# State @ W in two wide visits per batch, one x load on another queue, token sums on VectorE: a cross-attention plus GLU kernel on one core

## The chip, the cores and the metric

One core of a Trainium2 chip. The metric is the device time of one execution in microseconds (us), as the median of several executions. The profile's span is some 1.8 us shorter than the device time of the same execution (before: 232.0 for 233.72). TensorE is called PE in the profile, VectorE DVE, ScalarE ACT, GpSimd POOL, SyncE SP; PEld is the load of weights into TensorE.

## The reference, cut to what matters

```
# x: (8 batches, 8 heads, 512 tokens, 64), state: (8, 8, 32, 64), all float32
a     = softmax(x @ state.T / 8)          # each token over the 32 states
xread = a @ state
a2    = softmax(state @ x.T / 8)          # each state over the 512 tokens
sread = a2 @ x
y     = concat(xread, sread)  ->  (8 * 544, 512)
out   = (sigmoid(y @ w_gate) * (y @ w_val)) @ w_out     # 512 -> 1536 -> 512
```

The kernel uses two identities. First, xread @ W = a @ (state @ W): so it makes SW = state @ W of a batch (a small matmul, 64x32 tiles of the array, eight at a time) and multiplies it by aT. Second, both softmaxes share E = exp(x @ state.T / 8); the second one needs sums of E over the 512 tokens ("token sums").

## The kernel before: what the change touches

In the loop over batches, `b - 1` is at its output matmuls (`out_mm`), `b` at gate and value (`gv_mm`), and `nb = b + 1` is prepared: S and E, aT, token sums and sread (`sr_mm`), and SW (`sw_visit` on TensorE, `sw_cp` out of PSUM). PSUM has eight banks: gv 2, out 1 (`OU`), swp 4, attention 1 (`AT`). Names in code and traces: `xb` is x of a batch in bf16 and `xT` its transpose, which S needs; `ab` is the softmax a and `aT` its transpose, which gate and value multiply by SW; `res` is a block of out copied out of PSUM for its store. S is the product x @ state.T, E its exponential, sr the product for sread.

```python
    def sr_mm(b, place):                       # token sums, then sread, in one bank
        ...
        for e in range(2):
            for c in range(4):                 # 8 matmuls: 4 token groups x 2 head halves
                nc.tensor.matmul(sm, ones[:, e], Eb[:, c, e], start=(e == 0 and c == 0), stop=(e == 1 and c == 3))
        ... # 16 matmuls of sread

    def gv_mm(b, f, place):                    # 2 banks of gv: gate, value
        ... # 2 x 2 matmuls 128x512; then th = tanh(gate / 2) on ACT, glu = (th + 1) * value on DVE

    ... # start-up: batches 0 and 1, all weights and x of 0 to 3
    load_x(2, nc.gpsimd)
    load_wo(0); load_wo(1); load_wo(2)         # (three lines)
    ...
    pad(2, 6)
    load_x(3, nc.sync, 1, nc.gpsimd)           # SP, held until GpSimd gets here
    cast_x(2, pool, 0, 4)
    cast_x(2, pool, 4, 4)
    cast_x(3, pool, 0, 4)
    cast_x(3, pool, 4, 4)
    at_xT_dma(2)                               # 4 DMA transposes each, on SP
    at_xT_dma(3)

    for b in range(1, B + 1):
        nb = b + 1 if b + 1 < B else None
        if b == 1:
            for i in range(2):
                S_mm(nb, i, (AT, GV)[i])       # waits for the transposes of batch 2
                S_exp(nb, i)
                n_sum(nb, i)
                n_mul(nb, i, nc.vector)
            aT_dma(nb)
        for f in range(NF):                    # NF = 12
            if b < B or f < 9:
                out_mm(b - 1, f)
            if b > 1:
                gv_mm(b, f, SWP if b == B and f % 2 else GV)
                gv_th(b, f)
                gv_glu(b, f)
            if nb is not None:
                lo, q = f // 4 * 512, f % 4
                if q == 0:
                    sw_visit(nb, lo, 512, 0, 1)            # f = 0, 4, 8: four swp banks
                sw_cp(nb, lo, q // 2, q % 2, act)          # all twelve copies on ACT
                if f < 2 and b > 1:
                    S_mm(nb, f, AT)
                    S_exp(nb, f)
                elif f == 5:
                    sr_mm(nb, AT)
                    sr_fin(nb)
                ...
```

The softmax here doesn't subtract the row's maximum and nothing guards it: scores larger than these inputs give would overflow.

## Time and profile before

| | before |
|---|---|
| time, median (lowest to highest) of the first 4 executions | 233.35 us (232.95 to 233.52) |
| TensorE busy | 95% of the span |
| DVE, ACT, POOL busy | 52%, 60%, 18% |
| loop period (first visit of one batch to that of the next) | 24.11, 24.18, 24.26, 24.18 us |
| lost before the loop, waiting for transposes of batch 2 | 2.3 us |

The period is read from the starts of the first state @ W matmul of each batch in the timeline: 62.84, 86.95, 111.13, 135.39, 159.57. A timeline line reads: start, duration, engine, line of the kernel, operation, tile written <- tiles read, shape, how many; in brackets the idle time in front of it and what ended it.

### The profile page before, as it was taken

To read this page: it belongs to the slowest core of one execution; us is meant where nothing else is said; L and a number is where in the kernel's file an instruction comes from. 1 tells how busy PE (TensorE), PEld (TensorE's weight loads), DVE (VectorE), ACT (ScalarE), POOL (GpSimd) and SP (SyncE) were. 2 spreads that over 40 slices of the span, in tenths; PEclk is the share of its full clock that TensorE was granted. 3 is DMA by queue.
4 is the path that set the end of the run, shared out by engine and by line. 5 is a ranking of instruction groups with operands and counts; after the bars stand their busy time and mean duration, and the time that the engine had idled before them with its cause. 6 is when DMAs were issued, how large, how long until landed. Compare 5 with 4: busy or idle time off the path is not lost.

```text
span 232.0 us, 4595 instructions
## 1 busy us (share of the span) xinstructions
PE 220.8 (95%) x1784; PEld 110.9 (48%) x1784; DVE 120.3 (52%) x198; ACT 138.5 (60%) x258; POOL 42.6 (18%) x76
## 2 busy tenths in 40 slices
PE   7668999889999999999999999999999999999994
PEld 7553445344444444444445444544454444466754
DVE  2599889852157435753486339533763343332311
ACT  3677786555775677666765676567756644422411
POOL 1499720330041003300150006000200000000000
PEclk9799999999999999999999999999999999999999
DMA  6999999952956460644172721153113111112114
GB/s 210 351 185 186 251 246 243 137 105 45 269 157 188 105 148 29 212 102 118 45 226 54 129 94 45 37 124 113 48 34 103 48 45 45 45 61 77 45 33 107
DMA packets 38790, 28.09 MB, mean 121 GB/s; under 512 B 20976, under 2 KB 34160, under 8 KB 38768
## 3 DMA queue, kind: packets, MB, share of 16 engines
q1 hardware_dynamic: 33600, 22.49, 36.5%
q0 software_dynamic: 5024, 5.24, 13.3%
q8 instruction: 14, 0.23, 0.4%
q14 instruction: 8, 0.07, 0.1%
q10 hardware_dynamic: 144, 0.07, 0.1%
HBM read 18.35 MB, written 8.91 MB: 118 GB/s over the span
## 4 chain that ended last, share of the span: by engine, by line
PE 84%; DMA 6%; DVE 4%; SPq 3%; POOL 1%; issue 0%; DVEq 0%
PE outp L274 37%; PE gvp L246 31%; PE swp L212 5%; PE gvp L249 5%; DMA xf<-in_x_dram 4%; SPq L124 3%; DMA xT<-xb 3%; DVE ab L156 2%; PE Sp L130 1%; PE srp L193 1%; PE srp L190 1%; PE outp L293 1%; DVE rs L148 1%; POOL xb L99 1%; DVE ri L150 0%; SPq L78 0%
## 5 line engine op out<-in xcount | busy, mean ns | idle before, releaser
L261 DVE SCALAR_TENSOR_TENSOR glu<-th,gvp 128x512 bf16<-128x512 f32 (+1 forms) x108 | 70.2, 656 | 87.6 <-ACT th L256 68.5
L274 PE MATMUL outp<-wo,glu 128*128 128x512 bf16 x396 | 99.6, 379 | 0.0
L246 PE MATMUL gvp<-aT,SW 128*128 128x512 bf16 x384 | 96.5, 379 | 0.1
L256 ACT ACTIVATE th<-gvp 128x512 f32<-128x512 f32 (+1 forms) x108 | 61.4, 573 | 54.7 <-PE gvp L246 45.4
L246 PEld LDWEIGHTS <-SW 128*128 128x128 bf16 x384 | 37.0, 98 | 45.7 <-issue 2.8
L274 PEld LDWEIGHTS <-glu 128*128 128x128 bf16 x396 | 36.5, 98 | 43.2 <-issue 5.6
L232 ACT CAST SW<-swp 128x512 bf16<-128x512 f32 (+1 forms) x90 | 50.3, 580 | 6.0 <-PE swp L212 5.3
L278 ACT ACTIVATE res<-outp 128x512 f32<-128x512 f32 x33 | 19.7, 597 | 19.5 <-PE outp L274 19.5
L141 POOL CAST Eb<-E 128x256 bf16<-128x256 f32 x32 | 12.4, 429 | 101.8 <-ACT E L135 101.8
L99 POOL CAST xb<-xf 128x1024 bf16<-128x1024 f32 (+1 forms) x13 | 14.6, 1148 | 18.5 <-DMA xf<-in_x_dram 13.3
L156 DVE TENSOR_TENSOR ab<-E,ri 128x512 bf16<-128x512 f32 x14 | 14.7, 1051 | 0.1
L148 DVE TENSOR_REDUCE rs<-E 128x16 f32<-128x512 f32 x16 | 10.8, 676 | 2.3 <-ACT E L135 2.3
L135 ACT ACTIVATE E<-Sp 128x512 f32<-128x512 f32 x16 | 9.6, 609 | 2.7 <-PE Sp L130 2.6
L212 PE MATMUL swp<-wg,sTc 64*32 64x512 bf16 (+1 forms) x208 | 10.4, 369 | 0.0
L212 PE MATMUL swp<-wv,sTc 64*32 64x512 bf16 (+1 forms) x208 | 10.0, 361 | 0.2 <-POOL wv L90 0.2
L199 DVE RECIPROCAL r<-srp 128x128 f32<-128x128 f32 x8 | 7.6, 956 | 3.5 <-PE srp L193 3.5
L130 PE MATMUL Sp<-sTz,xT 128*128 128x64 bf16 x128 | 7.1, 198 | 2.5 <-DMA xT<-xb 1.6
L212 PEld LDWEIGHTS <-sTc 64*32 64x32 bf16 x416 | 4.1, 89 | 10.6 <-issue 10.1
L130 PEld LDWEIGHTS <-xT 128*128 128x128 bf16 x128 | 5.7, 101 | 6.9 <-issue 2.4
L249 PE MATMUL gvp<-XS,wg 128*128 128x256 bf16 x48 | 7.2, 273 | 0.0
L249 PE MATMUL gvp<-XS,wv 128*128 128x256 bf16 x48 | 7.2, 273 | 0.0
L307 PE MATMUL warm<-ident 128*128 128x128 bf16 x56 | 5.8, 290 | 1.4 <-POOL ident masks.py:199 1.4
(50 smaller groups left out, 92.3 us busy)
## 6 DMA issues: line engine op xcount, KB each, us to landing
out_dram<-res SPq DMA_DIRECT2D x31, 256.0 KB, 2.5
xf<-in_x_dram SPq DMA_DIRECT2D x6, 1024.0 KB, 6.7
wo<-in_moe_w_out_dram POOLq DMA_DIRECT2D x3, 512.0 KB, 17.7
xf<-in_x_dram SPq DMA_DIRECT2D x2, 512.0 KB, 5.4
wg<-in_moe_w_gate_dram POOLq DMA_DIRECT2D x2, 512.0 KB, 7.1
wv<-in_moe_w_val_dram POOLq DMA_DIRECT2D x2, 512.0 KB, 7.9
xf<-in_x_dram POOLq DMA_DIRECT2D x1, 1024.0 KB, 10.1
out_dram<-res SPq DMA_DIRECT2D x9, 64.0 KB, 1.7
```

Of the source, the lines that this page charges most:

```text
L99: cp(xbs[b].rearrange("p c h d -> p h c d")[:, lo:lo + n], xfs[b][:, lo:lo + n])
L130: nc.tensor.matmul(ps[:, c, :, jj], xTs[b][:, 2 * i + jj, c], sTz[:, b, 2 * i + jj], start=True, stop=True)
L148: nc.vector.tensor_reduce(rs, halfE(b, i), AX.X, ALU.add)
L156: eng.tensor_tensor(abs_[b].rearrange("p c e (j n) -> p (c e) j n", n=Ns)[:, :, 2 * i:2 * i + 2], halfE(b, i), ri.unsqueeze(3).to_broadcas ...
L212: nc.tensor.matmul(pss[e][j * Ns:(j + 1) * Ns, o:o + n], sTc[rows, b, j], (wg, wv)[w][rows, j, lo:lo + n], start=True, stop=True)
L232: cp(*sw_left.pop((b, lo, w, e)))
L246: nc.tensor.matmul(ps, SWs[b][:, g, w, fs], aTs[b][:, :, g], start=(g == 0), stop=(g == 1))
L249: nc.tensor.matmul(ps, (wg, wv)[w][:, j, fs], XS[:, j], start=(j == 0), stop=(j == 3))
L256: nc.scalar.activation(th, held["gv", b, f][0], AF.Tanh, scale=0.5)
L261: nc.vector.scalar_tensor_tensor(glus[b][:, f], held["th", b, f], 1.0, held["gv", b, f][1], ALU.add, ALU.mult)
L274: nc.tensor.matmul(ops[b, c], glus[b][:, f, c * 128:(c + 1) * 128], wo[:, f], start=(f == 0), stop=(f == NF - 1))
L278: nc.scalar.activation(res, ops[b, c], AF.Copy, scale=0.5)
```

## The change

Intent: TensorE is the bound, so give it less. Two visits of six banks in place of three of four save one change into and out of the tiled mode a batch; sums over the four token groups are added on DVE in fp32 and go to TensorE as two bf16 terms (value and remainder), so 4 matmuls in place of 8; x of batch 3 goes by ACT's DMA queue, so that SP's queue is free for the transposes.

```diff
+    def n_tok(b, e):
+        if e == 0:
+            held["E4", b] = ap_.tile((128, 2, 4, Ns), FP, name="E4")
+        nc.vector.tensor_reduce(held["E4", b][:, e].rearrange("p j n -> p (j n)"),
+                                E1s[b][:, :, e].rearrange("p c j n -> p (j n) c"), AX.X, ALU.add)
+    def n_split(b, k):
+        if k == 0:
+            Es[b] = ap_.tile((128, 2, 2, 4, Ns), BF, name="Es")
+            nc.vector.tensor_copy(Es[b][:, 0], held["E4", b])
+        else:
+            nc.vector.tensor_tensor(Es[b][:, 1], held["E4", b], Es[b][:, 0], ALU.subtract)
 ...  sr_mm: 4 terms from Es where there is one (batches 2 to 7)
+    def sw_wide(b, v):
+        ...
+        lo = 768 * v
+        for k, places in enumerate(((OU, AT), (SWP, SWP), (SWP, SWP))):
+            ...  k = 0: gate, 512 columns; k = 1: value, 512; k = 2: 256 of each
 ...
     gv_mm(1, 1, GV)
+    load_x(3, nc.scalar)
     gv_th(1, 1)
 ...
-    load_x(3, nc.sync, 1, nc.gpsimd)
 ...  in the loop:
+            v, q = f // 6, f % 6
+            if nb is not None and q == 0:
+                sw_wide(nb, v)                 # f = 0 and 6, ahead of gv_mm, and gv_mm ahead of out_mm
+                sw_cp(nb, v, 0, 0, act)
+                sw_cp(nb, v, 0, 1, act)
 ...  copies: two of the twelve on DVE; S at f = 1, 2; n_tok at 6, 7; n_split at 7, 8; sr_mm at 9; sr_fin at 10
 ...  out of batch 0 in the two gv banks, as OU is taken
```

More of the change, by code (lines that the diff above doesn't have):

```diff
@@ L65 @@
     xfs, xbs, xTs = {}, {}, {}
-    E1s, Ebs, abs_, aTs, SWs, glus = {}, {}, {}, {}, {}, {}
+    Es, E1s, Ebs, abs_, aTs, SWs, glus = {}, {}, {}, {}, {}, {}, {}
     vec, act, pool = nc.vector.tensor_copy, nc.scalar.copy, nc.gpsimd.tensor_copy
@@ L187, in sr_mm @@
         sr, sm = sr_parts(b)
-        for e in range(2):
-            for c in range(4):
-                nc.tensor.matmul(sm, ones[:, e], Eb[:, c, e], start=(e == 0 and c == 0), stop=(e == 1 and c == 3))
+        if b in Es:
+            terms = [(e, Es[b][:, k, e]) for e in range(2) for k in range(2)]
+        else:
+            terms = [(e, Eb[:, c, e]) for e in range(2) for c in range(4)]
+        for i, (e, rhs) in enumerate(terms):
+            nc.tensor.matmul(sm, ones[:, e], rhs, start=(i == 0), stop=(i == len(terms) - 1))
         for j in range(4):
@@ L194, in sr_mm, with sr_inv @@
                                  Eb[:, c, :, j], start=(c == 0), stop=(c == 3))
+    def sr_inv(b):
+        r2 = held["r2", b] = ap_.tile((128, 4, Ns), FP, name="r2")
+        nc.vector.reciprocal(r2, sr_parts(b)[1])
     def sr_fin(b):
-        sr, sm = sr_parts(b)
-        r2 = ap_.tile((128, 4, Ns), FP, name="r2")
-        nc.vector.reciprocal(r2, sm)
+        if ("r2", b) not in held:
+            sr_inv(b)
+        sr, r2 = sr_parts(b)[0], held["r2", b]
         for e in range(2):
@@ L229, in sw_visit @@
                 sw_left[b, lo, w, e] = (SWs[b][:, e, w, lo:lo + n], pss[e])
+    def sw_wide(b, v):
+        if b not in SWs:
+            SWs[b] = fp.tile((128, 2, 2, dff), BF, name="SW", bufs=2)
+        lo = 768 * v
+        for k, places in enumerate(((OU, AT), (SWP, SWP), (SWP, SWP))):
+            pss = [p[0].tile((128, 512), FP, name="swp", tag=p[1]) for p in places]
+            if k < 2:
+                sw_mm(pss, b, k, lo, 512, 0)
+            else:
+                for w in range(2):
+                    sw_mm(pss, b, w, lo + 512, 256, 256 * w)
+            for e in range(2):
+                if k < 2:
+                    sw_left[b, v, k, e] = (SWs[b][:, e, k, lo:lo + 512], pss[e])
+                else:
+                    sw_left[b, v, k, e] = (SWs[b][:, e, :, lo + 512:lo + 768], pss[e].rearrange("p (w n) -> p w n", w=2))
     def sw_cp(b, lo, w, e, cp):
@@ L270, in out_mm @@
         if f0 == 0:
-            place = SWP if b == B else GV if b == 0 and c % 2 else OU
+            place = SWP if b == B else GV if b == 0 else OU
             ops[b, c] = place[0].tile((128, 512), FP, name="outp", tag=place[1])
@@ L539 @@
         for f in range(NF):
-            if b < B or f < 9:
-                out_mm(b - 1, f)
-            if b > 1:
-                gv_mm(b, f, SWP if b == B and f % 2 else GV)
-                gv_th(b, f)
-                gv_glu(b, f)
+            v, q = f // 6, f % 6
[3 more added lines that the diff above has]
+                sw_cp(nb, v, 0, 1, act)
+            for first in (nb is not None and q == 0, nb is None or q > 0):
+                if first and b > 1:
+                    gv_mm(b, f, SWP if b == B and f % 2 else GV)
+                    gv_th(b, f)
+                    gv_glu(b, f)
+                elif not first and (b < B or f < 9):
+                    out_mm(b - 1, f)
             if nb is not None:
-                lo, q = f // 4 * 512, f % 4
                 if q == 0:
-                    sw_visit(nb, lo, 512, 0, 1)
-                sw_cp(nb, lo, q // 2, q % 2, act)
-                if f < 2 and b > 1:
-                    S_mm(nb, f, AT)
-                    S_exp(nb, f)
-                elif f == 5:
+                    sw_cp(nb, v, 1, 0, vec)
+                elif q in (1, 3, 4):
+                    k = {1: 3, 3: 4, 4: 5}[q]
+                    sw_cp(nb, v, k // 2, k % 2, act)
+                if f in (1, 2) and b > 1:
+                    S_mm(nb, f - 1, AT)
+                    S_exp(nb, f - 1)
+                elif f in (6, 7):
+                    n_tok(nb, f - 6)
+                    if f == 7:
+                        n_split(nb, 0)
+                elif f == 8:
+                    n_split(nb, 1)
+                elif f == 9:
                     sr_mm(nb, AT)
+                    sr_inv(nb)
+                elif f == 10:
                     sr_fin(nb)
-                    if b > 1 and nb + 1 < B:
+                if f in (2, 4) and b > 1:
+                    n_sum(nb, f // 2 - 1)
+                elif f in (3, 5) and b > 1:
+                    n_mul(nb, f // 2 - 1, nc.vector)
+                if f == 3:
+                    at_Eb(nb)
+                    if nb + 2 < B:
+                        load_x(nb + 2, nc.sync)
+                elif f == 5 and b > 1:
+                    aT_dma(nb)
+                    if nb + 1 < B:
                         cast_x(nb + 1, pool, 0, 4)
@@ L560 @@
                         at_xT_dma(nb + 1)
-                if f in (1, 3) and b > 1:
-                    n_sum(nb, f // 2)
-                elif f in (2, 4) and b > 1:
-                    n_mul(nb, f // 2 - 1, nc.vector)
-                if f == 2:
-                    at_Eb(nb)
-                    if nb + 2 < B:
-                        load_x(nb + 2, nc.sync)
-                elif f == 4 and b > 1:
-                    aT_dma(nb)
     for k in range(6):
```

## The prediction

> **What bounds the kernel now.** I began with the page: engine shares, then the chain that ended last.
>
> ```profile
> PE 220.8 (95%) x1784; PEld 110.9 (48%) x1784; DVE 120.3 (52%) x198; ACT 138.5 (60%) x258; POOL 42.6 (18%) x76
> PEclk9799999999999999999999999999999999999999
> PE 84%; DMA 6%; DVE 4%; SPq 3%; POOL 1%; issue 0%; DVEq 0%
> ```
>
> TensorE is busy 95% of the span at full clock and is 84% of the chain, so from about 50 us on the end moves by what TensorE is given or spared. Because a busy matmul row is a modelled length, I price TensorE by distances between starts, from the timeline. One batch in the middle (TensorE rows only):
>
> ```profile
> 156.89 1.03 PE L246 MATMUL gvp<-aT,SW 128*128 128x512 bf16 x4
> 157.75 1.03 PE L274 MATMUL outp<-wo,glu 128*128 128x512 bf16 x4
> 158.62 1.03 PE L246 MATMUL gvp<-aT,SW 128*128 128x512 bf16 x4
> 159.57 0.41 PE L212 MATMUL swp<-wg,sTc 64*32 64x512 bf16 x8
> 159.80 0.40 PE L212 MATMUL swp<-wv,sTc 64*32 64x512 bf16 x8
> 160.13 0.41 PE L130 MATMUL Sp<-sTz,xT 128*128 128x64 bf16 x8
> 160.38 0.81 PE L274 MATMUL outp<-wo,glu 128*128 128x512 bf16 x3
> ...
> 169.91 0.61 PE L190 MATMUL srp<-Eb,ones 128*128 128x128 bf16 x8
> 170.35 0.63 PE L193 MATMUL srp<-Eb,xb 128*128 128x64 bf16 x16
> 170.82 1.03 PE L274 MATMUL outp<-wo,glu 128*128 128x512 bf16 x4
> ```
>
> Four 128x512 matmuls take 0.865 us (157.75 to 158.62). The gv block at 158.62 would end at 158.62 + 0.865 = 159.485, but the first state @ W matmul starts at 159.57: 0.09 late. Its second group of eight follows after 0.23 (one group = one 512-column pass, as the eight 64x32 tiles run together), and S starts 0.33 after that, where a pass is 0.22. So one visit costs 160.13 - 159.485 = 0.645 us: two passes (0.45) and 0.20 for going into and out of the tiled mode. The token sums (8 matmuls) take 170.35 - 169.91 = 0.44, sr itself 0.47, each S 0.25. A batch: 24 x 0.865 + 3 x 0.645 + 0.44 + 0.47 + 2 x 0.25 = 24.1 us. The state @ W visits at 62.83 and 86.95 stand 24.12 apart: the loop has no stall to speak of, and only removed TensorE time counts there.
>
> The one large hole is before the loop. Chain from 40 to 49 us, then TensorE's rows and the DMA issues of that time:
>
> ```profile
> 41.49 5.83 DMA xT<-xb
> 47.32 0.05 issue
> 47.37 0.55 PE Sp L130 x13
> ```
> ```profile
> 42.63 2.54 PE L246 MATMUL gvp<-aT,SW 128*128 128x512 bf16 x11
> 45.86 0.20 PE L130 MATMUL Sp<-sTz,xT 128*128 128x64 bf16 x1 [0.69 <-DMA xT<-xb]
> ...
> 47.37 0.55 PE L130 MATMUL Sp<-sTz,xT 128*128 128x64 bf16 x13 [0.30 <-DMA xT<-xb]
> 47.76 1.03 PE L274 MATMUL outp<-wo,glu 128*128 128x512 bf16 x4
> ```
> ```profile
> 27.96 0.37 SPq L78 DMA_DIRECT2D xf<-in_x_dram  x1
> 35.16 8.25 SPq L124 DMA_TRANSPOSE xT<-xb  x4
> ```
>
> The last gv pass ends at 42.63 + 11 x 0.216 = 45.0. Sixteen S matmuls at 0.029 (0.47/16, from sr) would end at 45.46; out starts at 47.76. So 2.3 us are lost waiting for the transposes of batch 2. These sit behind the x load of batch 3 on SP's queue: issued at 27.96, it took 14.3 us (its maximum of issue to landing), to 42.3. The four transposes took 8.25 us to issue, against 5.04 for four later.
>
> **What the Trainium skill says.** (1) "TensorE: Matmul & The Clock Gate", "Wait — 56ns, not 53.3ns?": warm starts are 55.6 ns apart at N = 128 and 215.7 at N = 512. The trace agrees: 0.44/8 = 55, 0.865/4 = 216. (2) "TensorEngine Tiling (Array Packing)", "Key Properties": a change of tiling mode drains TensorE. The trace agrees, at about 0.20 us a visit. (3) "DMA: Bandwidth & Descriptors", "Queues, rings and completion order": an engine takes descriptors of one ring in order and goes round between rings; SP and ACT have one each. The trace fits: batch 2's transposes landed only after x of batch 3. (4) "VectorE: DVE Perf Modes", "The perf-mode tier table": tensor_reduce and fp32 tensor_tensor go at one element a cycle, an fp32 copy in SBUF at two. The trace: a 512-element reduce 0.676, the fp32-to-bf16 copy of 512 elements 0.43.
>
> **The change part by part.** It concerns the six batches (2 to 7) prepared in the loop.
>
> Visits: three of two passes become two of three. The passes stay six: the last 512 columns of a wide visit are two times 256 of gate and val, which start 0.11 apart in the start-up (16.47, 16.58, 16.68). A wide visit is 0.645 + 0.225 = 0.87; two are 1.74 against 1.935: 0.2 less a batch, one pair of drains. Six batches: 1.2 us.
>
> Token sums: 4 matmuls in place of 8, 4 x 0.055 = 0.22 less. Six batches: 1.3 us. DVE pays for it: two reduces of 512 (1.35), a 256-element copy (estimated 0.3 from the 0.43 and 0.69 of 512 and 1024) and a 256-element fp32 subtraction (estimated 0.42 from 0.68 for 512). Two SW copies of 0.68 also move from ACT to DVE. DVE so goes from 13.2 to about 16.6 us of a 23.7 us batch, ACT from 16.2 to 15.0. Neither becomes the bound in sum.
>
> X of batch 3: the ACT queue takes it at about 29.9 (just before the th at 30.24, where ACT idles 0.35), not SP at 27.96. I estimate 0.4 for the issue, so about 0.1 us of delay on ACT. The transposes then issue from about 34.5 at 1.26 each (5.04/4), to 39.6; with some 3 us to land and DMA still full, they should be there by 43 to 45, about when TensorE comes. Of the 2.3 us most should go. But 0.6 is given back at once: the first wide visit writes bank AT, which S of batch 2 has just filled, so it must wait for the exponential. In the trace that ended at 48.33, 0.57 after out could start; in before an out into another bank stood there. Net 1.5 with a little for the ACT issue and for transposes that are still late.
>
> Banks and order: a wide visit now takes the only out bank, after its evacuation. Around the visit the margins are small. The res copy runs 157.09 to 157.69, and a wide visit would write at 157.84. The gv pair of banks is reused every 1.735 us, as before (0.865 + 0.87). At the S steps, f = 1 and 2, ACT has th, SW copy, E, res, th in a row. Adding 0.6 each from the moment S is ready, res ends 0.05 before out needs the bank, and the glu behind it ends within 0.05 of the next val pass. Then n_mul, 1.42 us where it lies beside GpSimd's casts, can push a glu 0.2 too far. I allow 0.1 us of new stall a batch, 0.5 in all.
>
> Sum: 1.2 + 1.3 + 1.5 - 0.5 = 3.5 us. 233.5 - 3.5 = 230.0.
>
> **The rivals.** (a) The hole before the loop moves instead of closing. X of batch 3 starts 2 us later and shares the engines, so it may land at 44 to 46. SP runs in order: batch 3's four transposes wait for its cast (2.0 us), and the four aT transposes of batch 2 stand behind them. Landing at 45.5 gives 45.5 + 2.0 + 5.1 + 5.1 + 2.3 = 60.0 for aT, and the first gv of the loop would want it at about 59.8. For it: DMA is saturated from 18 to 48 us (share above 1), so order changes but work doesn't. Against: some 0.7 us of slack if x lands at 44.5. It would make the time 231 to 231.5. (b) DVE becomes the pacemaker: it has about 1.04 us between two glu, and n_tok with the SW copy needs 1.36. Against: that falls where two out blocks stand together, so 0.87 more is there. If it stalled TensorE 0.4 a batch, 232. (c) No stall appears and the start-up wait goes altogether: 2.5 + 2.3 - 0.6 = 4.2, or 4.8 if AT's wait is hidden too: 228.7 to 229.3.
>
> **Range and chances.** The 2.5 us of removed TensorE time is arithmetic from start distances; the start-up gain (0 to 2.3) and the new stalls (0 to 2) are not. So 228.6 to 231.8. Over 2% is below 228.84, which takes rival (c) whole: 0.16. Slower by 2% would need stalls of 8 us: 0.01.
>
> **What would show it.** Right: six passes a batch as before, and a wide visit of 0.87; token sums of 0.22 ahead of sr; the batch period at 23.7 to 23.8; transposes of batch 2 issued in about 5 us and S at 45 to 46; an AT wait of about 0.6 after it. Wrong: a period near 24.1 (stalls ate the saving; look at glu's wait before val passes), a wait for aT at the first gv of the loop (rival a), or ACT blocked for over 1 us by its DMA issue.

## The result, and the profile after

After: 230.91 us median of 4 (230.49 to 231.25); before, of the same rounds, 233.35. Ratio 0.9897 (95% interval 0.9874 to 0.9920). Ratios here and below are taken by machine from the fast runs of both kernels in the same rounds, so they are not quite the ratios of the medians. The predicted 230.0 is 0.9 too low; the range, 228.6 to 231.8, holds the result.

The page after: shares of the engines, then the chain.

```profile
PE 218.5 (96%) x1856; PEld 113.0 (49%) x1856; DVE 141.4 (62%) x234; ACT 131.2 (57%) x246; POOL 42.5 (19%) x75
PE 78%; DMA 10%; POOL 6%; SPq 3%; issue 1%; ACT 0%; DVE 0%; POOLq 0%; ACTq 0%
```

TensorE is still the bound, DVE took on 21 us as expected. One batch in the loop after, TensorE rows of the timeline:

```profile
83.08 1.03 PE L286 MATMUL gvp<-aT,SW 128*128 128x512 bf16 x4
84.03 0.41 PE L234 MATMUL swp<-wg,sTc 64*32 64x512 bf16 x8
84.26 0.40 PE L234 MATMUL swp<-wv,sTc 64*32 64x512 bf16 x8
84.47 0.29 PE L234 MATMUL swp<-wg,sTc 64*32 64x256 bf16 x8
84.58 0.29 PE L234 MATMUL swp<-wv,sTc 64*32 64x256 bf16 x8
84.81 1.04 PE L286 MATMUL gvp<-aT,SW 128*128 128x512 bf16 x4
...
103.43 0.39 PE L208 MATMUL srp<-Es,ones 128*128 128x128 bf16 x4
103.66 0.63 PE L211 MATMUL srp<-Eb,xb 128*128 128x64 bf16 x16
```

The wide visit costs 84.81 - (83.08 + 0.865) = 0.865 us, as predicted (0.87). The half passes are 0.11 apart. The token sums take 0.23 (predicted 0.22). The first visits of five batches stand at 60.38, 84.03, 107.67, 131.31 and 154.94: a period of 23.64 us, 0.54 less than the mean of 24.18 before, while the two removed pieces come to 0.43. So no new stall appeared, and some 0.1 us of old ones went. Waits of this size stand in the timeline before: in the batch from 86.95 on, a gv block starts at 94.03 and the visit behind it at 95.08, 1.05 later; elsewhere that distance is 0.95 or 0.96 (158.62 to 159.57). After, the same place reads 94.78 to 95.74.

Now the hole before the loop, after:

```profile
43.64 2.11 PE L286 MATMUL gvp<-aT,SW 128*128 128x512 bf16 x9
45.58 0.22 PE L130 MATMUL Sp<-sTz,xT 128*128 128x64 bf16 x2
46.02 0.20 PE L130 MATMUL Sp<-sTz,xT 128*128 128x64 bf16 x1 [0.21 <-DMA xT<-xb]
46.51 0.55 PE L130 MATMUL Sp<-sTz,xT 128*128 128x64 bf16 x13 [0.28 <-DMA xT<-xb]
46.99 0.39 PE L234 MATMUL swp<-wg,sTc 64*32 64x512 bf16 x1
47.57 0.41 PE L234 MATMUL swp<-wg,sTc 64*32 64x512 bf16 x7 [0.20 <-ACT E L135]
```

The last gv pass ends at 43.64 + 9 x 0.216 = 45.58. Sixteen S matmuls without a wait would end at 46.05, and the visit would begin at about 46.1. It begins at 46.99 (0.9 lost to the transposes) and stops after one matmul until 47.57, as the second one writes AT (0.58 lost to the exponential). So 1.5 us are lost where 2.3 were: 0.8 won, not 1.5. The DMA issues show why, SP's transposes first, then ACT's load:

```profile
35.13 7.21 SPq L124 DMA_TRANSPOSE xT<-xb  x4
29.41 0.43 ACTq L78 DMA_DIRECT2D xf<-in_x_dram  x1
```

The four transposes still took 7.21 us to issue (8.25 before; I had expected 5), though x of batch 3 is now on another queue.

The balance of the two profiled executions. From the end of the hole to the end of the span: before 232.0 - 47.76 = 184.24, after 228.7 - 47.57 = 181.13, so 3.1 us in six batches. The hole: 0.8. The first S stood 0.58 later than it could before (45.58 against 45.0), with the same instructions on TensorE up to there: the second half of x of batch 0 landed 0.6 later in this execution (GpSimd's cast of it at 8.3 against 7.7). 3.1 + 0.8 - 0.6 = 3.3, which is 232.0 - 228.7. The medians differ by 2.4 only: of the executions at hand the profiled one of after was the fastest, and that of before (233.72) the slowest.

### The profile page after: what moved, and what is told of

It reads as the page before. It is cut to its first block, busy times and chain, and to the rows that moved or that the text cites. A ratio compares the mean times of both kernels' runs of the same rounds, so it can differ in the third digit from the quotient of the medians.

```text
span 228.7 us, 4759 instructions
## 1 busy us (share of the span) xinstructions
PE 218.5 (96%) x1856; PEld 113.0 (49%) x1856; DVE 141.4 (62%) x234; ACT 131.2 (57%) x246; POOL 42.5 (19%) x75
## 4 chain that ended last, share of the span: by engine, by line
PE 78%; DMA 10%; POOL 6%; SPq 3%; issue 1%; ACT 0%; DVE 0%; POOLq 0%; ACTq 0%
PE outp L314 37%; PE gvp L286 28%; DMA xf<-in_x_dram 8%; PE gvp L289 5%; PE swp L234 4%; SPq L124 3%; DMA xT<-xb 2%; POOL Eb L141 1%; PE srp L211 1%; PE outp L333 1%; PE Sp L130 1%; POOL wg L83 1%; POOL ab L171 1%; POOL xb L99 1%; POOL wv L90 1%
## 5 line engine op out<-in xcount | busy, mean ns | idle before, releaser
L314 PE MATMUL outp<-wo,glu 128*128 128x512 bf16 x396 | 97.8, 379 | 0.0
L286 PEld LDWEIGHTS <-SW 128*128 128x128 bf16 x384 | 36.2, 98 | 45.1 <-issue 4.2
L314 PEld LDWEIGHTS <-glu 128*128 128x128 bf16 x396 | 37.5, 98 | 41.0 <-issue 0.4
L272 ACT CAST SW<-swp 128x512 bf16<-128x512 f32 (+1 forms) x78 | 42.2, 579 | 2.9 <-PE swp L234 1.6
L272 DVE CAST SW<-swp 128x512 bf16<-128x512 f32 x20 | 13.4, 683 | 2.7 <-PE swp L234 2.7
L171 DVE TENSOR_TENSOR ab<-E,ri 128x512 bf16<-128x512 f32 x14 | 13.7, 980 | 0.1
L156 DVE TENSOR_REDUCE E<-E 128x128 f32<-128x512 f32 x12 | 12.3, 1033 | 0.0
L234 PE MATMUL swp<-wg,sTc 64*32 64x256 bf16 (+1 forms) x256 | 11.9, 328 | 0.2 <-ACT E L135 0.2
L234 PEld LDWEIGHTS <-sTc 64*32 64x32 bf16 x512 | 6.2, 91 | 10.4 <-issue 7.7
L234 PE MATMUL swp<-wv,sTc 64*32 64x256 bf16 (+1 forms) x256 | 10.4, 324 | 0.2 <-POOL wv L90 0.2
## 6 DMA issues: line engine op xcount, KB each, us to landing
xf<-in_x_dram ACTq DMA_DIRECT2D x1, 1024.0 KB, 14.8
```

Of the source, the lines that this page charges most:

```text
L156: nc.vector.tensor_reduce(held["E4", b][:, e].rearrange("p j n -> p (j n)"), E1s[b][:, :, e].rearrange("p c j n -> p (j n) c"), AX.X, ALU.add)
L171: eng.tensor_tensor(abs_[b].rearrange("p c e (j n) -> p (c e) j n", n=Ns)[:, :, 2 * i:2 * i + 2], halfE(b, i), ri.unsqueeze(3).to_broadcas ...
L234: nc.tensor.matmul(pss[e][j * Ns:(j + 1) * Ns, o:o + n], sTc[rows, b, j], (wg, wv)[w][rows, j, lo:lo + n], start=True, stop=True)
L272: cp(*sw_left.pop((b, lo, w, e)))
L286: nc.tensor.matmul(ps, SWs[b][:, g, w, fs], aTs[b][:, :, g], start=(g == 0), stop=(g == 1))
L314: nc.tensor.matmul(ops[b, c], glus[b][:, f, c * 128:(c + 1) * 128], wo[:, f], start=(f == 0), stop=(f == NF - 1))
```

## The experiments

Twelve kernels ran, and all gave correct results. Beside each call the kernel before ran again: 9 to 11 executions each. These made plain what the first four had hidden: before has two groups of times. Of the 42 executions, 13 lie at 235.0 to 236.2 (6 of 11, 3 of 11, 3 of 11 and 1 of 9), and 28 of the others at 232.6 to 234.4 (one at 234.8). All of them count as fast runs. The ratios below hold both groups and are wide for that reason; where a tenth of a microsecond matters I read the period in the profile. In the first call, which tests the parts, six of the eleven are in the upper group. Against the mean of its lower five alone (233.56) the means of wide_only, tok_only, x_act_only and x_sp are faster by 0.4, 0.3, 0.0 and 1.7 us. Their own executions can hold the slow stretch too, so neither comparison is clean.

### Each part alone

**wide_only**: the wide visits alone (with the new order of blocks and the two SW copies on DVE that came with them).

```diff
 # from the changed kernel
-    load_x(3, nc.scalar)
+    load_x(3, nc.sync, 1, nc.gpsimd)     # at its old place
-                elif f in (6, 7): n_tok(...) ... n_split(...)
```

> The changed kernel with the token sums as before (8 matmuls a batch) and x of batch 3 on SP again: the wide visits alone. Theory: two visits save one pair of drains, 0.21 us a batch, 1.25 us in six, and the first wide visit of the loop gives back 0.5 to 0.6 by waiting for bank AT behind the exponential: 0.7 us faster than before, loop period 23.9 us. Rival (nothing is lost to AT because the wait falls into the wait for the transposes): 1.25 faster.

Measured: 233.05 us (232.42 to 233.87), ratio 0.9938 (0.9892 to 0.9983). Period 23.86 (62.78 to 158.23 in four), 0.32 less than before: 0.21 for the pair of mode changes and again some 0.1 of small stalls (whether the visits or the new order took these away wasn't separated). The AT wait is there (47.48 to 48.06), so the rival's "nothing lost to AT" is wrong. This profile shows something else. Its columns after the busy times of the five engines are the granted clock, the DMA share and GB/s:

```profile
48.00:49.00 1.00, 0.94 (x32) 0.50 (x32) 0.85 (x2) 0.98 (x3) 0.44 (x2) 0.96 0.69 136
49.00:50.00 1.00, 0.78 (x2) 0.29 (x2) 0.96 (x3) 1.00 (x3) 1.00 (x2) 0.50 1.89 123
50.00:51.00 1.00, 1.00 (x4) 0.39 (x3) 0.93 (x3) 0.08 (x1) 0.45 (x2) 0.50 0.29 5
51.00:52.00 1.00, 1.00 (x4) 0.34 (x3) 1.00 (x2) 0.00 (x0) 0.00 (x0) 0.50 0.03 4
52.00:53.00 1.00, 1.00 (x5) 0.44 (x4) 0.05 (x1) 0.00 (x0) 0.00 (x0) 0.84 0.26 56
```

After the hole (44.84 to 48.06) TensorE ran at half clock for (0.04 + 3 x 0.5 + 0.16) / 0.5 = 3.4 us, which costs 1.7 us. The profile of before (hole 45.0 to 47.76) shows no such stretch there; its only one is in the start-up, from 8.0 to 11.5 us.

**tok_only**: on the kernel before, the token sums alone.

```diff
 # from the kernel before
+                elif f in (6, 7): n_tok(nb, f - 6); n_split(nb, 0) at 7
+                elif f == 8: n_split(nb, 1)
-                elif f == 5: sr_mm(nb, AT); sr_fin(nb)
+                elif f == 9: sr_mm(nb, AT); sr_inv(nb)
+                elif f == 10: sr_fin(nb)
```

> The kernel before with only the token sums on DVE and sr moved from f = 5 to f = 9. Theory: 4 matmuls of 0.055 us less a batch, so 0.22 a batch, 1.3 us faster, although n_tok took 1.03 us and not 0.68. Rival: with DVE's extra 3 us a batch some glu comes late and the period shrinks by less than 0.15 us (under 0.9 us in all).

Measured: 233.27 us (232.50 to 234.14), ratio 0.9939 (0.9888 to 0.9990). Period 23.95 (62.71 to 158.49 in four): 0.24 less, the theory's figure (0.22) and no stall against it. DVE's work cost TensorE nothing that the period shows, although the reduce is dearer than I took it to be (page of the changed kernel):

```profile
L156 DVE TENSOR_REDUCE E<-E 128x128 f32<-128x512 f32 x12 | 12.3, 1033 | 0.0
L148 DVE TENSOR_REDUCE rs<-E 128x16 f32<-128x512 f32 x16 | 10.8, 678 | 0.9 <-ACT E L135 0.9
```

Both read 512 fp32 values a partition. The token sum reads them 1 KB apart and writes 128 results; the other reads neighbours and writes 16. Which of the two makes the difference wasn't separated.

**x_act_only**: on the kernel before, the x load alone.

```diff
 # from the kernel before
     gv_mm(1, 1, GV)
+    load_x(3, nc.scalar)
     gv_th(1, 1)
-    load_x(3, nc.sync, 1, nc.gpsimd)
```

> The kernel before with only x of batch 3 on the ACT queue. Theory: the transposes of batch 2 land about 0.9 us earlier (47.3 to 46.5 in the two profiles), nothing is given back as an out block follows S: 0.6 to 0.9 us faster. Rival: the DMA engines are full either way, the order hardly matters: within 0.3 us of before.

Measured: 233.55 us (232.87 to 234.35), ratio 0.9957 (0.9910 to 1.0004). In the profile out starts at 46.91 (47.76 before): 0.85 us earlier, as the theory says, with S possible at the same time (45.08, before 45.0) and the transposes issued in 6.69 us. The time doesn't resolve it, as the interval reaches from 2 us faster to no change.

**x_sp**: the changed kernel without the x move.

```diff
 # from the changed kernel
-    load_x(3, nc.scalar)
+    load_x(3, nc.sync, 1, nc.gpsimd)     # at its old place
```

> The changed kernel with x of batch 3 back on SP where it was. Theory: it keeps the loop's saving (period 23.64) and loses what the ACT queue gave: 2.0 us faster than before, against 2.44 for the whole change. Rival (the ACT queue was worth my predicted 1.5 us and more): 1 us or less faster than before.

Measured: 231.57 us (230.86 to 233.42), ratio 0.9885 (0.9834 to 0.9935), so about 2.7 us faster than before, as much as the whole change within the interval. The period is 23.64. The profiled execution, the slowest (233.42), has the half-clock stretch again, from 49.2 to 52.6. The rival, a start-up gain of 1.5 us and more, would leave 1 us or less here. The interval (1.5 to 3.9 us) excludes that, and so does the comparison with the lower group (1.7): the loop carries the gain.

### What keeps the hole open

**after_again**: the changed kernel, as yardstick.

> The changed kernel once more, as the yardstick for the three runs beside it. Both theories: 2.2 to 2.7 us faster than before, and the loop period 23.64. The start of the first gv block varies by some 0.5 us with the landing of x of batch 0.

Measured: 231.25 us (229.84 to 232.41), ratio 0.9867 (0.9808 to 0.9926). The gv block that the profile of after has at 17.66 came at 18.44 here: half clock lasted from 8.0 to 14.8 us in the start-up, against 9.8 to 13.2. The period is 23.64, as expected, and no half clock follows the hole (46.38 to 49.52).

**at_last**: the first wide visit takes AT last.

```diff
 # from the changed kernel
-        for k, places in enumerate(((OU, AT), (SWP, SWP), (SWP, SWP))):
+        order = ((SWP, SWP), (SWP, SWP), (OU, AT)) if last else ((OU, AT), (SWP, SWP), (SWP, SWP))
+        for k, places in enumerate(order):
...
-                sw_wide(nb, v)
+                sw_wide(nb, v, b == 1 and v == 0)
```

> The changed kernel, with the first wide visit of the loop taking the four swp banks first and OU and AT last, so that the exponential of S has 0.5 us to free AT. Theory: 0.5 us faster than the changed kernel, no wait of TensorE on E before the visit. Rival: the out block behind, or the SW copies, wait instead: no faster.

Measured: 230.64 us (229.64 to 232.51), ratio 0.9847 (0.9792 to 0.9903), 0.6 below after_again by median, which the spread doesn't resolve. The profile does: S ends its last group at 47.13 + 0.4, the visit starts at 47.61 and out at 48.53, 0.92 later where 0.78 is usual (84.03 to 84.81). So of the wait of 0.58 some 0.14 is left, now in front of the last pair of banks.

**x_late**: x of batch 3 behind the transposes of batch 2 on SP.

```diff
 # from the changed kernel
-    load_x(3, nc.scalar)
...
+    at_xT_dma(2)
+    load_x(3, nc.sync)
     cast_x(3, pool, 0, 4)
     cast_x(3, pool, 4, 4)
-    at_xT_dma(2)
-    at_xT_dma(3)
...
             aT_dma(nb)                       # of batch 2
+            at_xT_dma(3)
```

> The changed kernel with x of batch 3 on SP behind the transposes of batch 2, and the transposes of batch 3 behind those of aT of batch 2. Theory (x of batch 3 takes DMA time from the transposes on whichever queue it is): the transposes issue in 5 us and land by 43, S runs without a wait at about 45, 0.9 us faster than the changed kernel; x then lands at 46 to 47, in time. Rival (the expert weights on GpSimd's queue fill the engines, x is not the cause): the transposes land at 46 to 47 as now. Second rival: batch 3's transposes land too late for S of batch 3 (63 us), and the gain is lost there.

**x_late_at_last**: both edits.

> Both of these together. Theory: 1.4 us faster than the changed kernel (0.9 and 0.5), 3.8 faster than before. Rival: one hides the other, so no better than the better of the two.

Measured: x_late 237.13 us (233.93 to 238.57), ratio of the fast runs 1.0081 (1.0007 to 1.0154), its profiled run slow. (One of its six, at 233.93, is 2.6 us below the next; it wasn't profiled and stays unexplained.) x_late_at_last 236.50 (236.43 to 237.94), ratio 1.0110 (1.0057 to 1.0162). Both slower than before. Timeline of x_late_at_last, TensorE, then SP's issues:

```profile
44.91 0.63 PE L130 MATMUL Sp<-sTz,xT 128*128 128x64 bf16 x16
65.29 1.01 PE L287 MATMUL gvp<-aT,SW 128*128 128x512 bf16 x2 [5.26 <-ACT res L319]
```
```profile
35.60 5.39 SPq L124 DMA_TRANSPOSE xT<-xb  x4
41.04 0.58 SPq L78 DMA_DIRECT2D xf<-in_x_dram  x1
49.55 5.05 SPq L192 DMA_TRANSPOSE aT<-ab  x4
54.71 5.14 SPq L124 DMA_TRANSPOSE xT<-xb  x4
59.94 1.20 SPq L321 DMA_DIRECT2D out_dram<-res  x1
```

The theory's first half is shown: with x of batch 3 behind them, the transposes issue in 5.39 us, and all sixteen S matmuls run at once at 44.91. x_late shows the same (5.35 us, sixteen matmuls at 44.89). So what held them up in both kernels was the traffic of x of batch 3, on whichever queue. The loss comes from a wait that I hadn't foreseen, and not at S: SP's queue runs in order, the first store of a result stands behind eight transposes until 59.94, and as there are three res buffers the fourth evacuation waits, and TensorE behind it for 5.26 us. Half clock adds to it: it set in at 63.15, 3.1 us into this wait, and lasted to 70.0, so that 4.7 us of the work after the wait ran at half speed, some 2.3 us more.

### The two groups of times, and a version that closes the hole

**before_warm**: TensorE kept busy in the hole.

```diff
 # from the kernel before
         if b == 1:
+            warm(32, OU)                     # 32 matmuls of ident with ident, 128 columns
             for i in range(2):
                 S_mm(nb, i, (AT, GV)[i])
```

> The kernel before with 32 idle 128-column matmuls (1.8 us) put in front of S of batch 2, that is into the hole in which TensorE waits for the transposes. Theory: the two groups of times of the kernel before (233.2 to 233.7 and 235.4 to 236.1 in the last two calls) are runs without and with some 3.4 us at half clock after that hole, which costs 1.7 us. With TensorE busy in the hole the upper group goes: no run above 234.5, the median at 233.4, the lower group where it was. Rival: the upper group comes from elsewhere (start, DMA) and stays in about a third of the runs.

Measured: 233.40 us (233.18 to 233.85), ratio 0.9965 (0.9922 to 1.0007). The kernel before beside it: 233.32 to 236.23, with three of eleven above 235. Here 6 of 6 lie in the lower group, whose place didn't move. That is weak: with 13 of 42 in the upper group, chance alone would do it in (29/42)^6 = 11% of such sixes, and with the 3 of 11 of this call in (8/11)^6 = 15%. The mean granted clock of every execution is on record too. One stretch of 3.4 us at half speed lowers it by 0.007 (3.4 / 2 / 232), to 0.993. None of the 13 upper executions is above 0.993, while nine of the 29 lower ones are at 1.000. So each upper one holds time at a lower clock somewhere. That isn't enough by itself, as the other 20 lower ones lie at 0.990 to 0.993: in the profile of before the stretch is in the start-up. With the half-clock stretches behind the hole in wide_only and x_sp, where the profile shows their 1.7 us directly, I take the cause as likely, not shown; no upper execution of before itself was profiled.

**out_first**: the AT wait removed in another way.

```diff
 # from the changed kernel
+            if b == 1 and f == 0:
+                out_mm(0, 0)
             if nb is not None and q == 0:
                 sw_wide(nb, v)
```

> The changed kernel, with the first out block of the loop in front of the first wide visit, so that AT is free by the time that the visit comes. Theory: TensorE waits for no exponential there, 0.5 us faster than the changed kernel (at_last beside it, in the last call, was 0.6 by median), about 3.0 us faster than before's lower group. Rival: the time only moves to the next wait, no change.

Measured: 230.83 us (230.36 to 232.25), ratio 0.9869 (0.9818 to 0.9919). In the profile S (46.39), out (46.78) and the visit (47.74) follow without a wait on E. Against the changed kernel of another call (231.25) it is 0.4 lower, inside the spread. Four executions lie at 230.4 to 230.8, two at 231.7 and 232.3.

**x_late_pe**: x of batch 3 late, and SP's queue relieved.

```diff
 # from out_first
-    load_x(3, nc.scalar)
...
+    at_xT_dma(2)
+    load_x(3, nc.sync)
     cast_x(3, pool, 0, 4)
     cast_x(3, pool, 4, 4)
-    at_xT_dma(2)
     at_xT_dma(3)
...
-            aT_dma(nb)                       # b == 1 only
...
                 if f == 3:
+                    if b == 1:
+                        aT_mm(nb, OU)        # 8 transposes on TensorE
+                        aT_cp(nb, None, vec)
                     at_Eb(nb)
```

> x of batch 3 on SP behind the transposes of batch 2, as in x_late, but aT of batch 2 made by TensorE (8 transposes, 0.44 us) and not by DMA, so that SP's queue is free for batch 3's transposes and for the stores; the first out block ahead of the wide visit. Theory: S of batch 2 runs at once at 45 us as in x_late (hole of 1 to 3 us gone), no wait for a res buffer behind SP's queue (the 5.8 us of x_late), 0.44 paid: 1.4 to 1.9 us faster than out_first, 228.9 to 229.5, and with a smaller spread, as no hole drops the clock. Rival: batch 3's transposes come too late for S of batch 3, or something else on SP's queue stalls: no faster than out_first.

Measured: 229.62 us (229.33 to 229.78), ratio 0.9800 (0.9759 to 0.9842): 1.2 below out_first, and a spread of 0.45 us where out_first has 1.9. All sixteen S matmuls run at once at 44.96. TensorE waited 0.41 us for ab in front of the transposes.

**x_late_pe4**: these transposes one block later.

```diff
 # from x_late_pe
-                    if b == 1:               # at f == 3
-                        aT_mm(nb, OU)
-                        aT_cp(nb, None, vec)
+                elif f == 4 and b == 1:
+                    aT_mm(nb, AT)
+                    aT_cp(nb, None, vec)
```

> x_late_pe with the eight aT transposes one block later (f = 4, into AT), as TensorE waited 0.41 us for ab there. Theory: 0.2 to 0.4 us faster, 229.2 to 229.4, spread again under 0.6 us, period 23.64. Rival: the copy of aT out of PSUM now ends after the second wide visit wants AT, which gives 0.3 back: no change.

Measured: 228.98 us (228.81 to 229.35, 5 runs), ratio 0.9798 (0.9761 to 0.9835), before 234.01 in the same rounds. It is the best version, by median 0.6 below x_late_pe (on another chip, so that difference isn't resolved). TensorE's timeline where the hole was:

```profile
44.83 0.63 PE L130 MATMUL Sp<-sTz,xT 128*128 128x64 bf16 x16
45.30 1.03 PE L314 MATMUL outp<-wo,glu 128*128 128x512 bf16 x4
46.25 0.41 PE L234 MATMUL swp<-wg,sTc 64*32 64x512 bf16 x8
...
50.49 0.61 PE L178 MATMUL aTp<-ident,ab 128*128 128x128 bf16 x8
```

No idle time is left in it: S at 44.83, out at 45.30, the visit at 46.25, and the transposes without a wait.

## Why the prediction was right or wrong, point by point

- **Bound.** Right. TensorE stays at 96%, and what it was spared in the loop is what the end moved by.
- **Visits, 1.2 us, and sums, 1.3 us.** The mechanism was right and the sizes slightly low: a visit costs 0.865 (0.87 said) and the sums 0.23 (0.22 said). By the periods of the kernels with one part each they are worth 6 x 0.32 = 1.9 and 6 x 0.24 = 1.4; together 6 x 0.54 = 3.2.
- **New stalls, 0.5 us.** Wrong, in sign. The step "I allow 0.1 us of new stall a batch" failed: no margin around the S steps or the wide visits gave way, and about 0.1 us a batch of old waiting went with the wide visits. That "the loop has no stall to speak of" rested on one pair of visits, the shortest (24.11; the others 24.18 to 24.26).
- **DVE.** Right that its larger load stays beside TensorE; n_tok was mis-sized, 1.03 us for 0.68. It was covered, as two out blocks stand together at f = 6 and 7.
- **The start-up, 1.5 us.** This is the term that was mis-sized: 0.8 in the profile. The step "the transposes then issue from about 34.5 at 1.26 each (5.04/4), to 39.6 ... they should be there by 43 to 45" failed. They issued from 35.13 to 42.3, and the last S came at 46.51. I had laid the delay to the order in SP's ring; x_late_at_last shows that it is the traffic itself, as the transposes issue in 5.39 us only once x of batch 3 comes after them. My own rival (a) had the reason in hand ("DMA is saturated from 18 to 48 us (share above 1), so order changes but work doesn't") and I applied it to x, not to the transposes.
- **AT wait, 0.6 us.** Right: 0.58 (the exponential's end, 48.33 in the prediction, is 47.78 + 0.60 = 48.38 in the trace), mostly gone in at_last and wholly in out_first.
- **Rivals.** (a) did not come: x of batch 3 landed at 29.41 + 14.8 = 44.2, and the first gv of the loop (61.17) had no wait for aT of batch 2. (b) did not come. (c) came true in the loop, where no stall appeared, and not in the start-up.
- **The sum.** 3.2 + 0.8 would be 4.0. The profiled pair has 3.3, with 0.6 lost to a later start. The medians of the first rounds have 2.4. So part of the closeness to 230.0 is luck: the loop gave 3.2 where 2.0 was predicted (1.2 + 1.3 - 0.5), the start-up 0.8 where 1.5 was, and the medians hold 1.6 less than these two parts together. That remainder isn't pinned down: the executions spread by 0.6 us before and 0.8 after, and starts at half clock vary the start-up. What I had left out is that an execution can lose 1.7 us to half clock behind the hole, as wide_only and x_sp did.

## What to carry to other kernels

Price a TensorE-bound loop by distances between starts; removed passes and removed mode changes then came out to a few hundredths of a microsecond a batch, and small waits moved the period by another 0.1. When DMA is full, moving a transfer to another queue may help little the one that is waited for (0.8 of 2.3 us here); putting the less urgent one behind it took the whole wait away, once nothing else stood behind in the same in-order queue. Close a wait of some 3 us on TensorE even where it looks small: here it cost 1.7 us of half clock afterwards in two profiles, and where it was closed the times spread by 0.5 us in place of 1.9.

## What the Trainium skill lacked or had wrong

- "TensorEngine Tiling (Array Packing)", "Key Properties", says that a mode switch drains, with no number. Here going in and out cost 0.20 us a visit.
- "TensorE: Matmul & The Clock Gate", "HAM oscillation — how this bites in real kernels", gives idle gaps of more than about 3.4 us as the limit. Here holes of 3.2 and 3.5 us (wide_only 44.84 to 48.06, x_sp 45.39 to 48.91), which weren't even idle throughout, were followed by half clock for 3.4 us; two of 3.1 us (after_again 46.38 to 49.52, tok_only 44.73 to 47.85) weren't, and in x_late_at_last half clock set in 3.1 us into a wait. So the figure is near, a little high for these runs; so few holes fix no threshold. What the page doesn't say is how it may look in times: two groups about 2 us apart (likely, not shown).
- "DMA: Bandwidth & Descriptors", "Rules for kernel authors", says that spreading DMAs over issuing engines doesn't help bandwidth. The runs agree; what the rules lack is that the order in time does help the transfer that is waited for: four transposes took 7.4 to 8.8 us to issue with x of batch 3 ahead on their queue (five profiles), 6.7 to 7.4 with it on ACT's (five), and 5.4 to 6.2 with it behind them (four).
- "VectorE: DVE Perf Modes", "The perf-mode tier table", has one tier for tensor_reduce. Here two reduces of 512 fp32 values took 0.68 and 1.03 us, by read distance or by number of results (not separated).
